# Block-sparse attention with a gated convolution FFN on one core: three stores change their queue, five are split, and the last 17 of 41 lines of a written-out order are replaced

## The chip, the core and the metric

One core of a Trainium2 chip. Its engines run instruction streams of their own and meet only at semaphores: TensorE (PE: matmuls; PEld its weight loads), VectorE (DVE), ScalarE (ACT), GpSimd (POOL) and SyncE (SP), which here only issues transfers and DMA transposes. The metric is the device time of one execution in microseconds (us), lower is better. Times of the trace count from the start of the profiled span.

## The reference

Four batches, eight heads, 768 tokens, head width 64. A query block of 32 tokens sees its neighbours, the first and last block and three drawn blocks; the softmax over those keys is followed by an FFN whose gate is a convolution over three tokens.

```python
scores = np.where(mask, scale * np.matmul(q, k.transpose(0, 1, 3, 2)), -1e9)
attn = np.exp(scores - np.max(scores, axis=-1, keepdims=True))
attn = attn / (np.sum(attn, axis=-1, keepdims=True) + 1e-09)
x = np.matmul(attn, v).transpose(0, 2, 1, 3).reshape(B, S, H * D)
h = np.maximum(x @ w_in, 0.0)
...
for k in range(K):
    conv_out += conv_w[k][None, None, :] * hp[:, k:k + S, :]
gate = 1.0 / (1.0 + np.exp(-conv_out))
out = h * gate @ w_out
```

## The kernel before

**Attention.** The heads are handled in 16 pairs (0 to 15, four to a batch). A unit is 1024 columns of scores, 144 units in all. PE writes a unit's scores into one of two PSUM buffers `st` in two halves of 512 columns (L773; the mask rides along as 24 more rows of the contraction), ScalarE takes their exponential into one of six buffers `pt` (L785), and PE multiplies that by the values in eight matmuls of 65 columns (L810). A unit's buffer `st` is free for the unit after next when its exponential is done. VectorE divides by the sums (`rcp` L719, `xtok` L721).

**FFN.** Tokens come in nine segments: 0 to 6 of 384 tokens (segment 4 is the first half of batch 2), then 7 (256 tokens) and 8 (128 tokens) for the second half of batch 3. For each, the attention's output is transposed (by DMA from SP, L730, for segments 2 to 6; by PE, L740, and a copy for 0, 1, 7 and 8), multiplied by `w_in` into one of two PSUM buffers `mix` (L910, called f1 here), and put through a relu on ScalarE (L930) or VectorE (L932). Segments 0 to 6 have eight groups g0 to g7 of one f1 and one relu each; 7 and 8 have four, g0 to g3. The gate takes four pairs p0 to p3 of feature chunks per segment: three multiplies (L968) and two adds (L976) on VectorE, a tanh on ScalarE (L1015), an add of one (g1, L1018) and a multiply (g2, L1023) on VectorE. In segment 8 the convolution runs on PE instead (L987, two steps per pair) with its tanh at L992.

**Output.** An output tile (b, t) is 128 tokens of batch b. It takes eight matmuls in four steps (L844, called f2 here; one step needs the g2 of one pair), is copied out of PSUM by ScalarE (L324) or VectorE (L328) into one of four buffers `o2s`, and stored (L854). Tiles (3,3), (3,4) and (3,5) are made in column pieces. A buffer of `o2s` is free again when its store has landed.

**The order.** No scheduler runs. The text `ORDER` (L20 to L61) lists all 1811 steps, two characters for the step, one for the engine where there is a choice, one for each buffer taken; `put_down` reads it and records the steps, so each engine's stream is exactly the list's order for that engine, and a step that waits holds up all behind it on its engine. A transfer's issue is a step of SP, ACT or POOL. `OUT_POOL` (L219) names three tiles whose store POOL issues; the others go to SP, and the third piece of a tile to ACT.

The loads of keys (`nat`), queries and values (`vn`) are issued by POOL (L239) in order; between them stand 1x1 copies (`pace`, L419) that wait for a given unit's exponential, so that loads start no sooner. Values go on by a copy to `vt` (L328) on VectorE.

Of the kernel before, what the change touches and what calls it, by code (L numbers as in the profile page):

```python
# [40 lines left out]
414213/24643lic41lplwlx3OVlqcj2lF1lz0cm0cnlGlAcu1cvcw1co4lBlHly3YV1lIlJV3cz1lClDV0cAcfcB3cE0lO1cFlPlL03ZVc540V1lQV  # L41
cG0lMlNAcgcJ1cKm70cO0cPckcllU1cpcqlVm8m9macr0cL5lR0lSmbcscQ2lWAlTAmf1mccx0cW1cycXcCc/0cDl+1l/d0cHcIcMcNcY4d41d5d13
d65mhmgmdmim0VcRcT2mjlX0lYcS1lZAcZd90c+m11dadh1d2dim40d3m2d7mkdb2dj3dm0dnm5d8dr1ds44454c4f4g04k4h4imemn2momlmqcUm3V
m6VmpkolKc61471lE4l048cVctdo1mJ1dcdw0dxdddk0dldt0dy4mv3mxmrmmmwde1mydfmzdB1dCdpmD0dqdJ0dKdumKdD5msdL3mA4t4u24d04y4j
mtdO1dvdPdzdAmEmudEdF1dT0dMdUdNmLmF49V2mBmCdQ1dV0dRdY1dSdZmMe40d+44bdge5e65dWmGmNV1mHV2dG2e91eadXd/eb3dH4eV2n21n3e0
e10e2ee0efeg1ej1m/0n0eke70e8n1A084aVn4V4mnn0nonq4nV3dI2e34z1mO4v4w4H4q4I34r1el0eo0ecepeq24M4x4E4F24J4K4Ledn50n6eh
n81n9ein7A9ew1exnb0nceB0ey5naVeCeD3emne1nfngAeG1eHeI14S4T0enereL0eMeN4nk1es1ezeAeEeFeJeKnleT1eUeOeP4oVndVanv1npnx
et1nD2nrnEeunwnseV0nmAeQ2eRnGnF4p4A4N0eSev4Onh0nieY0eZf11f2eW0njAbe+2nL3nynzmP1mQf35nAmRf60mV0f7f83eXmSe/fb1mWfcf0
f4f5mXfj0mYfk4sV34GV4nHnMntnI4BV4nOnNnPnu04CVfd4mTA3mZA0fl1nQfo1f9faoc1odo30feff1o4oeVnBnJo91fpfmfnft0oao5Afq0o60fu
o7fy1fzobAfg0nRnKfhnCnZ1fv2oz0oBnSo8Aor2oAosouotn+fG0oi0fHfA5fI3n/o0fL1fMo1A1fN4frfQ0fsof1fwfRfS1fxogfV1fWojohAfX0  # L50
ov4PV04QVoCfBfCfD2okVfJ0fKfOf+0f/ol1g61oo0g7opoH1oI4UV0g02owgb0gcfPfTfUfYfZfEoJoDoqVg85gd3oEg1g21omgg1g9ghnT0nUgl0
gagmnVoKonVoxoyo2mUfi04DfFgi4gn1g31oP3g4oFoLoGoRoQnWnXA1gt1gugegy0p11gfoX0gzgv0oYgjgkgogD1gEp2oMgA2gF5oSoToNoUgpgq0
oOgrgw0gxgBgCgM0gNgR1gSp3gGgHoZgT3gO4oVoWg5m+gsnYo+p4gW1gI2gJo/V3p0gP1gXpd0h30h4pep5V04Rp6mIgY1pfgK1h50gLA1pgphV1
h81h9pj1pkpm0pngQhd0ha2plA1cpoApH2hehm1gUhf5pIpKpJpLhnho4ps1gVpp0gZptpqg+hr0puAprAdg/1pP0pRpQhshw1py1hxh60h7pzhbpv0
pwpMht3h0pSpAApNpxAehF0hGp71pB0pChchgp8hhhp1p9pahqpTpX1pYpZhH1pDAfpUhy0p+hK0hLh10huhvpbA3h2AhzhApE1pO1hi0pVhjp/hk0
pFhT1hI0hM2hB2hChlVhD0pGApWhEVq0hJhUi00qq1hNqri1hV5q33q4q5q6q1q7qsAgi24q8hO1qw0i51qxhWi6ie0ifqH2hP1q2hXqb1qcq9qahY0
qIig3qyAhhZhQqX0qZqYqdqeqn0i31qoi4i70i8qfA0qpAiia2qKi90ihhR1iihSA2ibij1qz1qAqBikq+qt0ic1quidAqh1qvAjqih+0qjh/Vil0qk
imAru0rvqCqJqDqlA2rl1rmrwAqErnAq/qP3qRqLqFqGrr0rsrtAqMqQqNrx1ryro1rz1rAqOrBqSrprqArH0r30rIrC1rDr0rJ2rE1qmqgpcpirKqT
rFr1rGqUrLqVqWr4r91rarM0s70sd1rNses8sfs9rO1r5rPr2rQr6r7A3sarbrcsgrR0rSsbV2rdA0rTrUshVrVA1r8rescsirWrf1rgrhrirjArk
rX0rYrZr+s10s2s3s4s5Ar/Vs0s6  # L60
"""  # L61


# [19 lines left out]
class Graph:  # L83
# [29 lines left out]
def kernel(  # L113
# [32 lines left out]
    def many(n, shape, dt, tag):  # L146
        return [sb.tile(shape, dt, tag=f"{tag}{x}", name=f"{tag}{x}") for x in range(n)]
# [21 lines left out]
    o2s_t = many(NOS, [128, DM], FP32, "o2s")  # L169
# [18 lines left out]
    op = gr.op  # L188
# [23 lines left out]
    def T(u):  # L212
        return T0 + PACE0 * u if u < 18 else T0 + 18 * PACE0 + PACE1 * (u - 18)

    SW = 0.715
    NWARM, NFILL = 13, 29
    SPLIT = ()
    X_PE = (0, 1, 7, 8)
    OUT_POOL = ((2, 5), (3, 0), (3, 1))  # L219
    WOUT_U = (15, 19, 23, 27)  # L220


# [11 lines left out]
    def on(e):  # L234
        return {"SP": nc.sync, "ACT": nc.scalar, "POOL": nc.gpsimd}[e]
# [11 lines left out]
    def first_k(x, e, prio, after):  # L247
# [7 lines left out]
        out=sbi[64:MR], in_=sampled_blocks.bitcast(I32).rearrange("b r -> (b r)").unsqueeze(0).broadcast_to([NB, 6 * NB])),  # L255
# [8 lines left out]
        out=ident, in_=ident, compare_op=ALU.not_equal, fill=1.0, base=0,  # L264
# [10 lines left out]
    def a_edges(e):  # L275
# [8 lines left out]
        out=nblk.rearrange("j (b t) -> j b t", t=32),  # L284
        in_=ident[0:NB, 0:NB].unsqueeze(2).broadcast_to([NB, NB, 32])), -14, [o_ident])
# [36 lines left out]
    def dcopy(e, dst, src):  # L322
        if e == "ACT":
            nc.scalar.copy(out=dst, in_=src)  # L324
        elif e == "POOL":
            nc.gpsimd.tensor_copy(out=dst, in_=src)
        else:
            nc.vector.tensor_copy(out=dst, in_=src)  # L328
# [45 lines left out]
    for s in range(NHE):  # L374
# [372 lines left out]
    for u, (n, blocks) in enumerate(units):  # L747
# [3 lines left out]
        for part in range(2):  # L751
# [17 lines left out]
            def s_fn(e, stb=stb, pieces=pieces):  # L769
                st = st_t[stb.index]  # L770
                for (P, hh, kc, idx, x, n_) in pieces:
# [6 lines left out]
                        uses=[slot_b[P] for P in sorted({h[0] for h in heads})] + ([stb] if part else []))  # L778
# [49 lines left out]
    def out_block(b, t, due, deps, after, tail=False, last=False):  # L828
        gb, ob = gt_buf[b], Buf(P_os)
        halves = {3: ((0, 256), (256, 512)), 4: ((0, 256), (256, 384), (384, 512)),  # L830
                  5: ((0, 256), (256, 512))}.get(t if b == B - 1 else 0, ((0, 512),))
        outs = []
        for x, (c0, c1) in enumerate(halves):
            tl = last or x == 2
            mb = Buf(P_tail if tl else P_mix)

            def acc(mb=mb, c0=c0, c1=c1, tl=tl):
                t_ = st_t[mb.index] if tl else mix_t[mb.index]
                return t_[:, 0:c1 - c0]
            prev = None  # L840
            for a in range(4):
                def fn(e, a=a, acc=acc, c0=c0, c1=c1):
                    for ffc in (2 * a, 2 * a + 1):
                        nc.tensor.matmul(out=acc(), lhsT=gT_t[gb.index][:, ffc, 128 * t:128 * t + 128],  # L844
                                         rhs=woutb[:, ffc, c0:c1], start=(ffc == 0), stop=(ffc == NFFC - 1),
                                         skip_group_check=True)
                prev = op("f2", {"PE": 2 * t_mm(c1 - c0)}, fn, due + 0.4 * a + 0.1 * x,
                          [ld_wout[a]] + deps[a] + (last_exps if tl and a == 0 else []),
                          after=[prev] if a else after, alloc=[mb] if a == 0 else [], uses=[gb] + ([mb] if a else []))
            evo = op("ev", {"ACT": t_act(c1 - c0), "DVE": t_dps(c1 - c0) + 0.06},  # L850
                     lambda e, acc=acc, c0=c0, c1=c1: dcopy(e, o2s_t[ob.index][:, c0:c1], acc()),
                     due + 2.5, [prev], alloc=[ob] if x == 0 else [], uses=[mb] + ([ob] if x else []))
            by = "POOL" if (b, t) in OUT_POOL else "ACT" if x == 2 else "SP"
            outs.append(op("out", {by: {"POOL": SW, "ACT": 0.1, "SP": 0.5}[by]}, lambda e, c0=c0, c1=c1: on(e).dma_start(  # L854
                out=out[b, 128 * t:128 * t + 128, c0:c1], in_=o2s_t[ob.index][:, c0:c1]),
                due + 3, [evo], uses=[ob], dma=("sw" if by == "POOL" else "hw", 0.72 * (c1 - c0) / 512 + 0.05)))

    def whole_gate(n, heb, gtb, base, W):

# [30 lines left out]
    for n, (b, g, tok, C, _) in enumerate(SEGS):  # L890
# [8 lines left out]
        for fg in range(NFFC // FB):  # L899
            hb = Buf(P_mix)  # L900
            due = base + W * 0.6 * fg * FB / 8
# [33 lines left out]
            for f in range(FB * fg, FB * fg + FB):  # L935
                if f % 2 == 0 and tok + w1 < S:
# [4 lines left out]
                   uses=[hb] + ([] if new else [heb]) + (  # L941
                       [near[(n - 1, f // 2)] for f in range(FB * fg, FB * fg + FB) if f % 2 == 0] if g else []))
# [129 lines left out]
```

## Time and profile before

| | |
|---|---|
| median of 3 runs (lowest to highest) | 207.52 us (206.97 to 207.55) |
| the profiled execution's own time | 207.34 us |
| its span, first to last instruction | 205.5 us (so 1.84 us lie around it) |
| granted TensorE clock | 1.00 |
| transfers over the span | 25.45 MB, 124 GB/s |

Busy time on PE counts a matmul up to its modelled end, about 0.16 us past the point where the next one starts, so short waits of PE do not show as idle time. They show in the timeline, where rows of one kind follow each other: the distance of two starts against the columns that lie between them. In a row that merges several instructions the second number runs from the first start to the last end.

### The profile page before, as it was taken

Reading aid. Unit: us, or ns where it says so; the run is one execution under the profiler, and the core shown is the slowest. Engines: PE = TensorE matmul, PEld = TensorE weight load, DVE = VectorE, ACT = ScalarE, POOL = GpSimd, SP = SyncE. Lnnn points to the kernel's source line nnn. Section 1 sums busy time; section 2 is a strip of 40 time slices with the busy share of each in tenths; the row PEclk is TensorE's granted clock in tenths of the full one; section 3 lists DMA queues with packets and bytes.
Section 4 is the critical chain, followed back from the end, with each engine's and each line's share of the span. In section 5 each row is a group of like instructions: output and inputs, shape, how many; then the busy total and the mean of one; then the engine's idle time right before and its main releaser. Section 6 shows DMA issues by size and latency. Waiting matters only on the chain.

```text
span 205.5 us, 6316 instructions
## 1 busy us (share of the span) xinstructions
PE 199.5 (97%) x2442; PEld 144.4 (70%) x2442; DVE 186.5 (91%) x580; ACT 188.9 (92%) x249; POOL 62.7 (30%) x119
## 2 busy tenths in 40 slices
PE   6899999999999999999999999999999999999993
PEld 4688877877677766766477767756676757796773
DVE  6899999999999998999899979999999947999970
ACT  5999999999999999999799998999999979998751
POOL 6986735235241514114114554900000000000300
PEclk9999999999999999999999999999999999999999
DMA  6999999999959986999869496992041260010216
GB/s 146 186 195 198 195 197 130 145 114 139 159 79 111 147 122 84 244 121 168 199 97 176 60 134 94 211 169 58 2 132 21 75 218 10 3 53 3 102 59 200
DMA packets 50001, 25.45 MB, mean 124 GB/s; under 512 B 35508, under 2 KB 47380, under 8 KB 49972
## 3 DMA queue, kind: packets, MB, share of 16 engines
q0 software_dynamic: 20240, 12.03, 45.7%
q1 hardware_dynamic: 29300, 12.66, 31.4%
q8 instruction: 19, 0.31, 0.6%
q10 hardware_dynamic: 432, 0.36, 0.5%
q14 instruction: 10, 0.08, 0.2%
HBM read 23.09 MB, written 6.29 MB: 143 GB/s over the span
## 4 chain that ended last, share of the span: by engine, by line
PE 74%; ACT 13%; DVE 9%; issue 3%; ACTq 0%
PE st L773 26%; PE mix L910 16%; PE mix L844 14%; PE av L810 13%; ACT pt L785 8%; DVE m L968 3%; DVE t L328 2%; ACT m L1015 1%; PE st L844 1%; DVE m L976 1%; DVE xtok L721 1%; ACT hE L930 1%; PE mix L740 1%; ACT o2s L324 1%; PE av L987 1%
## 5 line engine op out<-in xcount | busy, mean ns | idle before, releaser
L785 ACT ACTIVATE pt<-st 128x1024 bf16<-128x1024 f32 x144 | 140.4, 1032 | 5.2 <-PE st L773 3.9
L773 PE MATMUL st<-t 88*128 88x256 bf16 (+2 forms) x600 | 92.9, 267 | 0.9 <-ACT pt L785 0.3
L810 PEld LDWEIGHTS <-pt 128*128 128x128 bf16 x1152 | 55.4, 97 | 13.7 <-ACT pt L785 0.5
L773 PEld LDWEIGHTS <-t 88*128 88x128 bf16 x600 | 48.7, 97 | 21.0 <-issue 1.6
L810 PE MATMUL av<-vt,pt 128*128 128x65 bf16 x1152 | 62.5, 193 | 0.1
L910 PE MATMUL mix<-xT,winb 128*128 128x384 bf16 (+2 forms) x288 | 55.4, 307 | 0.2
L968 DVE TENSOR_SCALAR m<-hE,cw 128x382 bf16<-128x382 bf16 (+2 forms) x192 | 50.3, 321 | 1.7 <-ACT hE L930 1.5
L844 PE MATMUL mix<-woutb,gT 128*128 128x512 bf16 (+2 forms) x200 | 49.0, 360 | 0.0
L976 DVE TENSOR_TENSOR m<-m 128x764 bf16<-128x764 bf16 (+2 forms) x64 | 33.7, 532 | 0.5
L910 PEld LDWEIGHTS <-winb 128*128 128x128 bf16 x288 | 23.6, 97 | 8.2 <-issue 0.9
L1015 ACT ACTIVATE m<-m 128x764 bf16<-128x764 bf16 (+2 forms) x32 | 26.2, 822 | 0.6 <-DVE m L976 0.5
L844 PEld LDWEIGHTS <-gT 128*128 128x128 bf16 x224 | 18.9, 97 | 9.5 <-DVE gT L1023 1.1
L419 POOL COPY pace<-pt 1x1 bf16<-1x1 bf16 x24 | 8.9, 370 | 49.8 <-ACT pt L785 49.6
L854 POOL DMA_DIRECT2D out_dram<-o2s x3 | 1.8, 590 | 59.0 <-ACT o2s L324 59.0
L930 ACT ACTIVATE hE<-mix 128x384 bf16<-128x384 f32 (+2 forms) x39 | 18.9, 501 | 0.2 <-PE mix L910 0.2
L1023 DVE TENSOR_TENSOR gT<-m,hE 128x764 bf16<-128x764 bf16 (+3 forms) x36 | 18.0, 510 | 0.7 <-ACT hE L930 0.4
L721 DVE TENSOR_TENSOR xtok<-av,rcp 128x384 bf16<-128x384 f32 (+2 forms) x36 | 18.2, 507 | 0.3
L239 POOL DMA_DIRECT2D nat<-in_q_dram x23 | 16.8, 730 | 1.7 <-issue 1.0
L328 DVE COPY t<-mix 64x384 bf16<-64x384 bf16 (+1 forms) x34 | 13.8, 411 | 0.6
L932 DVE TENSOR_SCALAR hE<-mix 128x384 bf16<-128x384 f32 x25 | 13.7, 550 | 0.6 <-PE mix L910 0.3
L328 DVE COPY o2s<-mix 128x512 f32<-128x512 f32 (+1 forms) x11 | 7.1, 654 | 6.3 <-PE mix L844 6.2
L1018 DVE TENSOR_SCALAR m<-m 128x764 bf16<-128x764 bf16 (+3 forms) x36 | 11.8, 334 | 0.6 <-ACT m L1015 0.5
(76 smaller groups left out, 132.3 us busy)
## 6 DMA issues: line engine op xcount, KB each, us to landing
out_dram<-o2s SPq DMA_DIRECT2D x18, 256.0 KB
vn<-in_v_dram POOLq DMA_DIRECT2D x16, 192.0 KB, 5.2
nat<-in_k_dram POOLq DMA_DIRECT2D x15, 192.0 KB, 4.5
nat<-in_q_dram POOLq DMA_DIRECT2D x6, 192.0 KB, 4.9
winb<-in_moe_w_in_dram POOLq DMA_DIRECT2D x2, 512.0 KB, 6.7
woutb<-in_moe_w_out_dram POOLq DMA_DIRECT2D x4, 256.0 KB, 6.0
nat<-in_q_dram POOLq DMA_DIRECT2D x9, 96.0 KB, 5.0
out_dram<-o2s POOLq DMA_DIRECT2D x3, 256.0 KB, 2.7
```

What stands on the lines that cost most here:

```text
L328: nc.vector.tensor_copy(out=dst, in_=src)
L721: nm = op("norm", {"DVE": t_dps(128 * C)}, lambda e: nc.vector.tensor_tensor(out=xtok_t[xk.index][:, 0:C].rearrange("p c h d -> p h c d"), ...
L773: nc.tensor.matmul(out=st[:, 128 * x:128 * (x + n_)], lhsT=t[0:88, 12 + 6 * hh + kc, :], rhs=t[0:88, idx:idx + (n_ - 1) * (2 if P < NPE el ...
L785: nc.scalar.activation(out=pt_t[ptb.index][:, c0:c1], in_=st_t[stb.index][:, c0:c1], func=AF.Exp, bias=0.0, scale=0.125)
L810: nc.tensor.matmul(out=o[:, off:off + 65], lhsT=pt_t[ptb.index][:, 128 * x:128 * x + 128], rhs=V_t[vslot_b[P].index][:, hh, kc, 0:65], sta ...
L844: nc.tensor.matmul(out=acc(), lhsT=gT_t[gb.index][:, ffc, 128 * t:128 * t + 128], rhs=woutb[:, ffc, c0:c1], start=(ffc == 0), stop=(ffc == ...
L910: nc.tensor.matmul(out=mix_t[hb.index][:, w1 * y:w1 * y + w1], lhsT=winb[:, fc, 128 * ffc:128 * ffc + 128], rhs=xT_t[xt_buf[n].index][:, f ...
L930: nc.scalar.activation(out=dst, in_=src, func=AF.Relu, bias=0.0, scale=0.5)
L968: nc.vector.tensor_scalar(out=m_t[cb.index][:, x, y, 0:w], in0=hE_t[heb.index][:, f0 + y, t0 + x:t0 + x + w], scalar1=cw[:, x, f0 + y:f0 + ...
L976: nc.vector.tensor_tensor(out=m[:, a_, :, 0:w], in0=m[:, a_, :, 0:w], in1=m[:, b_, :, 0:w], op=ALU.add)
L1015: th = [op("tanh", {"ACT": t_act(2 * w) + 0.04}, lambda e, cb=cb, w=w: nc.scalar.activation(out=m_t[cb.index][:, 0, :, 0:w], in_=m_t[cb.in ...
L1023: nc.vector.tensor_tensor(out=gT_t[gtb.index][:, f0:f0 + 2, t0:t1], in0=m_t[cb.index][:, 0, :, 0:w], in1=hE_t[heb.index][:, f0:f0 + 2, 1 + ...
```

## The change

The stores of tiles (2,5), (3,0) and (3,1) are issued by SP instead of POOL. The stores of (0,1), (0,2), (1,0), (1,1) and (1,2), 256 KB each, become two of 128 KB (columns 0 to 255 and 256 to 511), issued one behind the other by SP. The order is the same up to step 1100 of 1811 (about 118 us into the profiled span of before) and another one from there; the same 356 steps stand on PE behind that point.

```diff
-    OUT_POOL = ((2, 5), (3, 0), (3, 1))
+    OUT_TWO = ((0, 1), (0, 2), (1, 0), (1, 1), (1, 2))
...
-            by = "POOL" if (b, t) in OUT_POOL else "ACT" if x == 2 else "SP"
-            outs.append(op("out", {by: {"POOL": SW, "ACT": 0.1, "SP": 0.5}[by]}, lambda e, c0=c0, c1=c1: on(e).dma_start(
-                out=out[b, 128 * t:128 * t + 128, c0:c1], in_=o2s_t[ob.index][:, c0:c1]),
-                due + 3, [evo], uses=[ob], dma=("sw" if by == "POOL" else "hw", 0.72 * (c1 - c0) / 512 + 0.05)))
+            cuts = (c0, (c0 + c1) // 2, c1) if (b, t) in OUT_TWO else (c0, c1)
+
+            def store(e, cuts=cuts):
+                for y0, y1 in zip(cuts, cuts[1:]):
+                    on(e).dma_start(out=out[b, 128 * t:128 * t + 128, y0:y1], in_=o2s_t[ob.index][:, y0:y1])
+            by = "ACT" if x == 2 else "SP"
+            outs.append(op("out", {by: 0.1 if by == "ACT" else 0.5 * (len(cuts) - 1)}, store, due + 3, [evo], uses=[ob],
+                           dma=("hw", 0.72 * (c1 - c0) / 512 + 0.05)))
```

In `ORDER` 17 lines of text (L44 to L60) are replaced; read back, they differ in these places among others ("exp 108" is unit 108's exponential, "s4 p0" segment 4, pair 0):

| engine, place | before | after |
|---|---|---|
| ACT, units 106 to 113 | exp 106, exp 107, tanh s4 p0, exp 108, relu s4 g7, relu s4 g6, exp 109, exp 110, tanh s4 p1, exp 111, tanh s4 p2, exp 112, copy (1,4), copy (1,5), exp 113 | exp 106, exp 107, exp 108, relu s4 g6, tanh s4 p0, exp 109, relu s4 g7, exp 110, tanh s4 p1, exp 111, tanh s4 p2, exp 112, exp 113, copy (1,5) |
| DVE, same place | both adds of s4 p1 behind the last multiply of p2 and the first of p3 | both adds of s4 p1 ahead of them |
| DVE, first steps behind 118 us | value copy of pair 12 between two divisions; value copy of pair 13 28 steps later | value copy of pair 12, two key copies, relu s4 g0, value copy of pair 13, division of s5 |
| POOL, from 115 us | pace, keys 14, values 12, pace, three pieces of queries, two paces, keys 15, values 13 | values 12, pace, keys 14, a piece of queries, pace, pace, values 13, queries, pace, keys 15 |
| PE, f1 of s7 g0 | f1 first half, 4 matmuls of unit 141, f1 second half | f1 in one go, then unit 141 |
| ACT, last units | exp 140, relu s7 g1, exp 141, tanh s6 p3, ... | exp 140, exp 141, relu s7 g1, tanh s6 p3, ... |
| PE, s8 | f1 g3, g0, g2, conv p0 (both), f1 g1, conv p2, f2 (3,2), conv p2, ... | f1 g0, g2, conv p0, f1 g3, conv p0, f1 g1, conv p2 (both), f2 (3,2), ... |
| ACT, s8 | relu s7 g2, copy of xT (hp 3), copy (3,1), relu g3, tanh s7 p0, relu g0, relu g2, tanh s7 p1 | relu s7 g2, copy of xT (hp 1), tanh s7 p0, copy of xT (hp 3), copy (3,1), relu g0, relu g2, tanh s7 p1, relu g3 |
| SP, last stores | (3,2), (3,3), (3,5), (3,5), (3,4), (3,3), (3,4) from 199.5 us on | (3,0), (2,4), (2,5), (3,1) ahead of (3,3), (3,2), (3,4), (3,5), (3,5), (3,3), (3,4) |

Behind step 1100, five copies of output tiles move from VectorE to ScalarE (three of 512 columns, two of 256) and two of 512 columns the other way.

More of the change, by code (lines that the diff above doesn't have):

```diff
@@ L43 @@
 d65mhmgmdmim0VcRcT2mjlX0lYcS1lZAcZd90c+m11dadh1d2dim40d3m2d7mkdb2dj3dm0dnm5d8dr1ds44454c4f4g04k4h4imemn2momlmqcUm3V
[L44 to L57, printed above, removed]
@@ L58 @@
-imAru0rvqCqJqDqlA2rl1rmrwAqErnAq/qP3qRqLqFqGrr0rsrtAqMqQqNrx1ryro1rz1rAqOrBqSrprqArH0r30rIrC1rDr0rJ2rE1qmqgpcpirKqT
-rFr1rGqUrLqVqWr4r91rarM0s70sd1rNses8sfs9rO1r5rPr2rQr6r7A3sarbrcsgrR0rSsbV2rdA0rTrUshVrVA1r8rescsirWrf1rgrhrirjArk
-rX0rYrZr+s10s2s3s4s5Ar/Vs0s6
+m6VmpkolKc61471lE4l048cVctdo1mJ1dcdw0dxdddk0dldt0dy4mv3mxmrmmmwde1mydfmzdB1dCdpmD0dqdJ0dKdumKdD5msdL3mEdO1dvdzdAdE
+dF1dPmtmu4d04t4u2mAdT0dUdMmFdNmLdgdQ1dV0dRdY1mBmCmMdZmGe40dSe5mNV1dG2d+4dWdXm/1e91n04eV249V24aVn1V084j4y4q4r1e65
+mHA2eaee0d/e0eb2n50efn21n34mmO4sV3dHe10e24z1dI2eg3ej1ekn6e70eo0epn4Vnn0n7V9np4nV3no4oVel1eq04v4H4I34w4x4E4M4J4F24K
@@ new lines @@
+4Lne1e8ew1ecexn80n9ey5edeheieB0nfeCemenereG1eHnaAeD2ngAnb0es1ezeL0nceMeAnh1nv1nqet1eI34S4T0eN1eunrndVanwnD2nxnEny
+eT1eEeUnk0eFnieJeKeOePeY0nleV4eZnjAbnseQ2eRnGnz4pe3ev4AeS4N04Oe+0eW0f11nmAf2mP1eXmQe/mRf60f0f7mV0f35f4mSnAf82fb1mW
+nFnL3nMnHnBntnOnNmTV3nP4GV44BV4nu0nCnIfcfd1fj0mXfkf5mYfl4fo1f9oc1fpft0odmZA0nQfq0oeVnJo90fafufeoao31obAfg0nK4CVo4
+o5Afy1fzo60o7nZ1n+oz0nRfv3fA5o8AoAnSfhoBor1otosoC4PV0ouoDov4QVfG0fHff1n/o0fI2fL1fMoi0fmfnfQ0fRo1A1ojfrof1ogfsfN1fw
+fxfV1fWfS4okAohAoEoH2owfX0nT0ol1fBfCfJ0f+0f/g03fKomfOfPnUg61fTg7g85nVoIoxonVoJoyoFoKgb0gcoo1opfUfD1oLfYfZgg1ghg1nW
@@ new lines @@
+oqVfE4UV0gd2o2fi0m+4b4DfFmU4RoMgi1oP3oQg32oGoRoSg4oTgl0gmg21gn4p11g9gt1gugagep2gfgjgy0gkgzgogv0nXA1gA3oUgpgw0gxoX0
+gD1gEgM0gBoYgF5gq0groNoOoVoWgNgCp3oZgR1gSgO2gGgHgP1o+gT1o/A0p4gW0gXgY4h31h4gI1gJp5V3gK0pd1pepfpgh80gLV1gsg5nYh9gQ
+h50phA1p0mIp6ha3pj0pm1pkpnplA1cpoApH1pIpJpKhd1hehf5hm0pp0ps1pqptgUhnhr1gVprAdpuAgZpy0g+h60h7ho2pLpMpP0g/0pQpRpNpSh0
+hbhspv1hw0pzhcht1hxpwhghhpAApxAepThi2pX2pYhjp+pO1pZhy4hF1pB0pChGp71p8pDAfp9hK0h10pahp1hLhqhuhvhH0pUpVp/h2ApbA0hzhA
+hk0hB1hlVpE1pFhM3hChT1hD0hUi00hI0hJpGApWhEVq33q0q4q5q6q1qq1hNhP0hO1i1qw0qrhV5i22qsAgq7q8hWq2i51i6hXhY2ie0ifqH1q9qb1
@@ L61 @@
+qxqcqdqaig1qyAhhZqIqX0hQqKqYqeqn0qoi31i4i74i8qfA2qpAii90hR1ihiihSA2ia1ibqz2qAqBqCij0qDikqt0ic1quidAqh1qvAjqih+0qj
+h/Ail0qkqEimAqlA3rl0rmrnAqP3qQqFqJqGqLq+qSqRrr1rsrtAqMrx1ru0rvryro1rprH0rwArz2qNqTrAqOqZrBrIr30rqArC1rDr4r91raqgpc
+piqmqUrE1rJ2q/qVr0rFqWrGr1rKrM1sd0s71rNrbr5s8serO3r2rLrPrcrQrdA2s9r6r7V0rR1rSsfrTrUsasgrf0rgrVA1sbA3shArer8rWscsirh
+rirjArkrX1rYrZr+s11r/Vs0s2s3s4s5As6
 """
```

## The prediction

> **What bounds the kernel now.** I read the page first, then the busy time by stage behind the point from which the two orders differ, then PE's timeline there.
>
> ```profile
> span 205.5 us, 6316 instructions
> PE 199.5 (97%) x2442; PEld 144.4 (70%) x2442; DVE 186.5 (91%) x580; ACT 188.9 (92%) x249; POOL 62.7 (30%) x119
> ...
> out_dram<-o2s POOLq DMA_DIRECT2D x3, 256.0 KB, 2.7
> ```
>
> ```profile
> 118.00:130.00 12.00, 12.00 (x147) 8.32 (x144) 10.52 (x26) 11.03 (x14) 6.50 (x12) 1.00 1.00 124
> ...
> 150.00:170.00 20.00, 20.00 (x228) 13.56 (x225) 16.35 (x44) 18.61 (x24) 0.00 (x0) 1.00 0.37 117
> ...
> 186.00:202.40 16.40, 16.04 (x176) 12.29 (x174) 13.16 (x56) 10.78 (x26) 1.75 (x3) 1.00 0.26 91
> 202.40:205.50 3.10, 0.00 (x0) 0.00 (x0) 0.00 (x0) 0.23 (x1) 0.00 (x0) 0.98 0.39 117
> ```
>
> The columns are PE, PEld, DVE, ACT and POOL busy, the clock, the transfers' share and GB/s. Of the stages shown PE has a hole in the last two alone, 0.36 us up to 202.4 and then 3.1 us in which the last store lands. The change takes no matmul away, so it can win only what PE loses between matmuls, which the busy time hides. PE's timeline shows it, in six places:
>
> ```profile
> 134.28 1.22 PE L773 MATMUL st<-t 88*128 88x128 bf16 x8
> 135.34 0.28 PE L810 MATMUL av<-vt,pt 128*128 128x65 bf16 x4
> ...
> 140.63 0.83 PE L773 MATMUL st<-t 88*128 88x128 bf16 x4
> 141.30 0.40 PE L810 MATMUL av<-vt,pt 128*128 128x65 bf16 x8
> ```
>
> ```profile
> 185.64 1.03 PE L844 MATMUL mix<-woutb,gT 128*128 128x512 bf16 x4
> 186.63 0.60 PE L910 MATMUL mix<-xT,winb 128*128 128x256 bf16 x4
> ...
> 188.16 0.28 PE L810 MATMUL av<-vt,pt 128*128 128x65 bf16 x4
> 188.52 0.60 PE L910 MATMUL mix<-xT,winb 128*128 128x256 bf16 x4
> ...
> 190.44 0.59 PE L844 MATMUL mix<-woutb,gT 128*128 128x512 bf16 x2
> ...
> 190.98 0.59 PE L844 MATMUL mix<-woutb,gT 128*128 128x512 bf16 x2
> 191.49 1.80 PE L910 MATMUL mix<-xT,winb 128*128 128x128 bf16 x24
> 193.37 0.50 PE L987 MATMUL av<-hE,diag 128*128 128x130 bf16 x6
> ```
>
> Four matmuls of 512 columns take 1.03 us and two 0.59, so a matmul costs (1.03 - 0.59) / 2 = 0.22 us for 512 columns, 0.42 ns a column, once its tail is left out. Against that price: the eight scores from 134.28 are four halves of a unit, 2048 columns or 0.86 us, and the next row starts after 1.06: **0.20 lost**. The four from 140.63 are 1024 columns, 0.43 of 0.67: **0.24**. The four f2 from 185.64 need 0.87 of 0.99: **0.12**. Four matmuls of 65 columns (0.03 each) from 188.16 need 0.12 of 0.36: **0.24**. Two f2 from 190.98 need 0.43 of 0.51: **0.08**. The 24 f1 of 128 columns need 1.29 of 1.88: **0.59**. Together 1.47 us, the ceiling of what a new order can win.
>
> **The change part by part.**
>
> *Stores to SP.* Three issues leave POOL, which does nothing from 150 to 170 us and only them behind 186 (1.75), and come to SP.
>
> ```profile
> L854 SPq DMA_DIRECT2D out_dram<-o2s x24: 332/412/575, 81.2 to 202.4; - x24
> ```
>
> ```profile
> 199.47 3.29 SPq L854 DMA_DIRECT2D out_dram<-o2s  x7
> ```
>
> At 0.41 us each that is 1.2 us of SP. SP's new stream has them ahead of the last seven, behind the copy of (3,0). That copy is done at 187.96 (its row, from 187.37, follows below) and SP's last seven begin at 199.47: cost nothing. Without that idle SP they would delay the last stores by 1.2 us at most. The buffers: (2,5) has its store now when (3,0) has been copied, about 188.5, and lands by 191.2 with the 2.7 of the page; the next user of a buffer comes at 198.5.
>
> POOL's issues could also have slowed VectorE beside them.
>
> ```profile
> 188.75 1.25 DVE L968 TENSOR_SCALAR m<-hE,cw 128x256 bf16<-128x256 bf16 x6
> ...
> 192.18 0.92 DVE L968 TENSOR_SCALAR m<-hE,cw 128x256 bf16<-128x256 bf16 x4
> ```
>
> ```profile
> 192.49 1.75 POOL L854 DMA_DIRECT2D out_dram<-o2s  x3 [59.00 <-ACT o2s L324]
> ```
>
> The multiplies under POOL's stores (from 192.49) take 0.23 each, those before them 0.21 (0.92 / 4 against 1.25 / 6): at most 0.08 us in four. I put it at zero. [...]
>
> *Split stores.* Five more issues at 0.41 us are 2.1 us of SP.
>
> ```profile
> 95.98 5.89 SPq L854 DMA_DIRECT2D out_dram<-o2s  x4
> 103.42 1.19 SPq L730 DMA_TRANSPOSE xT<-xtok  x1
> ```
>
> Four of the five lie here or just behind; after the row of four SP is free from 101.87 to 103.42, so three halves' 1.2 us just fit, and no transpose starts later. The bytes are the same. Cost between 0 and, if the gap did not hold, 0.4 for the transpose at 103.42; zero taken.
>
> *The order, first place (131 to 142 us).* Both losses there are scores that wait for an exponential.
>
> ```profile
> 131.10 1.95 ACT L785 ACTIVATE pt<-st 128x1024 bf16<-128x1024 f32 x2
> 133.10 0.84 ACT L1015 ACTIVATE m<-m 128x764 bf16<-128x764 bf16 x1
> 133.85 1.01 ACT L785 ACTIVATE pt<-st 128x1024 bf16<-128x1024 f32 x1
> 134.75 0.87 ACT L930 ACTIVATE hE<-mix 128x384 bf16<-128x384 f32 x2
> ...
> 137.63 0.84 ACT L1015 ACTIVATE m<-m 128x764 bf16<-128x764 bf16 x1 [0.19 <-DVE m L976]
> ...
> 140.01 1.02 ACT L785 ACTIVATE pt<-st 128x1024 bf16<-128x1024 f32 x1
> ```
>
> Exp 108 (133.85) stands behind a tanh, exp 112 (140.01) behind all of these and a wait for VectorE's add. In the new order exp 108 follows exp 107 at once. Start to start an exp takes 1.95 - 1.02 = 0.93, a tanh 133.85 - 133.10 = 0.75, a relu 0.37 (two in 0.87 with a tail of 0.50). From exp 107 (131.10 + 0.93 = 132.03): exp 108 starts at 132.96 and ends at 133.97, against 134.85 now, so unit 110's scores do not wait: 0.20 won. Up to exp 112 the new list has five exp, three tanh, two relu: 132.03 + 4.65 + 2.25 + 0.74 = 139.67, end 140.69, provided that the adds, which the new VectorE stream has two multiplies earlier, are there. PE wants it 0.24 + 0.20 earlier than the present end of 141.03, at 140.59, so up to 0.10 of the 0.24 may stay: 0.14 to 0.24 won. Sum **-0.4**; if the lead is lost again, 0.
>
> *Second place (182 to 188.5 us).* Exp 141 now goes ahead of a relu, so unit 143's scores, the relu of s7 g3 and f1 of s7 g0 and g2 come sooner. The losses of 0.12 and 0.24 hang on these relus:
>
> ```profile
> 187.37 0.59 ACT L324 COPY o2s<-mix 128x512 f32<-128x512 f32 x1
> 187.84 0.63 ACT L930 ACTIVATE hE<-mix 128x512 bf16<-128x512 f32 x1
> ```
>
> ACT's work between is unchanged, so of the second I take half: **-0.2**, bounds 0 and -0.36.
>
> *Third place, s8.*
>
> ```profile
> 191.17 0.27 ACT L324 COPY xT<-mix 128x128 bf16<-128x128 bf16 x1 [0.93 <-PE mix L740]
> 191.61 0.59 ACT L324 COPY o2s<-mix 128x512 f32<-128x512 f32 x1 [0.17 <-PE mix L844]
> 192.13 0.39 ACT L930 ACTIVATE hE<-mix 128x256 bf16<-128x256 f32 x1
> ```
>
> The first conv needs the relu of g0. Before, relu g3 (192.13) and a tanh go first, and conv starts at 193.37 behind three f1. In the new order g0's relu is the one at 192.13, done at 192.52. A tanh now stands ahead of the copy at 191.17, up to 0.5 us on f1 g0; but g2's bank is freed by the copy of (3,1), 192.20, in either order, so 0.2 of that is hidden and f1 g2 runs from 192.24 to 192.67. Conv starts there without a wait, f1 g3 follows, and at 193.10 the same work is done as before at 193.37: **-0.27**; bounds +0.1 (all of the tanh shows) and -0.59.
>
> *Copies that change engine.* ScalarE gets one 512-column copy more and two of 256, VectorE has these less: about 0.47 + 2 x 0.28 = 1.0 us by the distance of starts, 187.37 to 187.84 for the first and by columns for the others. They fall where ACT has room, 1.0 of 12, 1.4 of 20 and 5.6 of 16.4 us: nothing.
>
> The sum is -0.4 - 0.2 - 0.27 = -0.87. Some twenty other steps of PE have leads of 0.05 to 0.2 us in the new list by the same counting, so I give 0.17 back: **-0.7**. The profiled execution took 207.34 (205.5 and 1.84 around it), 0.18 under the median: 206.6 on its own scale, **206.8** against 207.52.
>
> **The rivals.**
>
> *Values come late (slower).* VectorE's stream now has the value copy of pair 13 in front of two divisions and the relu of s4 g1, not behind all these. By the count of PE's columns PE wants that relu's bank at 126.7.
>
> ```profile
> 124.07 0.35 DVE L328 COPY vt<-vn 128x768 bf16<-128x768 bf16 x1
> ```
>
> ```profile
> 118.88 0.61 POOL L419 COPY pace<-pt 1x1 bf16<-1x1 bf16 x1 [0.89 <-ACT pt L785]
> ...
> DMA to landing us min/median/max: 3.4/5.2/10.1
> ```
>
> That load is issued behind two paces, about 119.9. Copy, two divisions, a reciprocal and the relu take about 1.9, so it must land by 124.8: 4.9 us. At 3.4 nothing happens, at 5.2 PE loses 0.3, at 7 it loses 2.1 and the time is 208.9; slower than before from 5.6 on. For it: the median. Against it: no other load of that size is issued in the three us ahead, so I expect 4.2.
>
> *The leads do not hold:* waits come back elsewhere, above all behind the copies of (2,2) and (2,5) on ScalarE, 0.47 each: 207.1 to 207.7.
>
> *All six losses go:* -1.3: 206.2.
>
> *SP is late:* halves and stores push transposes back by 0.4 to 1.2: 207.3 to 208.2.
>
> **How the numbers follow.** Forecast 0.48, leads lost 0.20, values late 0.16, SP 0.08, all six 0.08. A difference of 0.3% (0.62 us) is what a measurement here can tell from none, so 206.9 is the edge: of the forecast 0.38 lie below it. Faster 0.46, same 0.33 (0.10 of the forecast, all of the lost leads, 0.03 of the late values), slower 0.21. The forecast's own range is 206.4 to 207.3; eight in ten need 206.1 (ceiling of 1.47) to 208.3 (part of the late values).
>
> **What would show it.** Right: scores of units 110 and 114 follow their predecessors without the 0.20 and 0.24; first conv of s8 directly behind f1 g2; last PE row ends near 201.6; SP has room before its last seven. Wrong: PE losing time at 126 to 128 with VectorE idle before a value copy; transposes at 103 us later than now; new losses between 142 and 182, where before has none.

## The result, and the profile after

| | median us | executions | ratio to before, 95% interval |
|---|---|---|---|
| before | 207.59 | 22 | |
| after | 206.95 | 22 | 0.9966 [0.9952, 0.9979] |
| after, measured once more (below: e6_again) | 207.04, before beside it 207.39 | 12 and 35 | 0.9991 [0.9974, 1.0008] |

By the medians the change wins 0.64 us in the first comparison and 0.35 in the second, whose interval does not rule out that nothing was won; 206.8 was forecast. The profiled execution of after took 207.02.

The page of after, first lines, and the busy time by stage (the columns as in the prediction):

```profile
span 205.2 us, 6315 instructions
PE 200.1 (98%) x2442; PEld 145.2 (71%) x2442; DVE 184.7 (90%) x577; ACT 189.4 (92%) x252; POOL 60.0 (29%) x116
```

```profile
186.00:202.40 16.40, 16.08 (x176) 12.35 (x174) 12.89 (x54) 11.20 (x28) 0.00 (x0) 1.00 0.30 108
202.40:205.20 2.80, 0.00 (x0) 0.00 (x0) 0.00 (x0) 0.09 (x1) 0.00 (x0) 0.83 0.42 126
```

POOL's 1.75 us of stores are gone from the last stages, and from 202.4 to the end it is 2.8 us, not 3.1. PE is as full as before; what changed is again between matmuls. PE's timeline of after at the two places of the first part, and ScalarE's:

```profile
135.28 0.60 PE L773 MATMUL st<-t 88*128 88x256 bf16 x4
135.72 0.60 PE L844 MATMUL mix<-woutb,gT 128*128 128x512 bf16 x2
...
141.11 0.38 PE L773 MATMUL st<-t 88*128 88x384 bf16 x2
141.33 0.28 PE L810 MATMUL av<-vt,pt 128*128 128x65 bf16 x4
```

```profile
131.49 2.92 ACT L785 ACTIVATE pt<-st 128x1024 bf16<-128x1024 f32 x3
...
139.97 1.96 ACT L785 ACTIVATE pt<-st 128x1024 bf16<-128x1024 f32 x2
```

Unit 110's scores (135.28) take 0.44 to the next row, the price of 1024 columns; the first half of unit 114's (141.11) takes 0.22 for 512. The 0.20 and 0.24 are gone: exp 106, 107 and 108 run in a row of three. The last stage:

```profile
185.30 1.46 PE L844 MATMUL mix<-woutb,gT 128*128 128x512 bf16 x6
186.67 1.03 PE L914 MATMUL mix<-xT,winb 128*128 128x256 bf16 x8
...
188.11 0.40 PE L810 MATMUL av<-vt,pt 128*128 128x65 bf16 x8
188.56 0.60 PE L914 MATMUL mix<-xT,winb 128*128 128x256 bf16 x4
...
191.06 0.59 PE L844 MATMUL mix<-woutb,gT 128*128 128x512 bf16 x2
191.68 1.25 PE L914 MATMUL mix<-xT,winb 128*128 128x128 bf16 x16
192.77 0.33 PE L991 MATMUL av<-hE,diag 128*128 128x130 bf16 x3
```

The first convolution (192.77) follows its f1 at once. Six f2 take 1.37 where 1.29 are needed (0.08 lost, 0.12 before), the eight from 188.11 0.45 for 0.24 (0.21, was 0.24), two f2 0.62 for 0.43 (0.19, was 0.08), 16 f1 1.09 for 0.86 (0.23; 24 lost 0.59 before). And two losses above 0.1 us are new:

```profile
119.54 0.29 PE L810 MATMUL av<-vt,pt 128*128 128x65 bf16 x4
119.83 0.60 PE L844 MATMUL mix<-woutb,gT 128*128 128x512 bf16 x2
...
158.15 0.29 PE L810 MATMUL av<-vt,pt 128*128 128x65 bf16 x4
158.45 0.60 PE L773 MATMUL st<-t 88*128 88x256 bf16 x4
```

Four matmuls of 65 columns cost 0.12; here 0.29 and 0.30 pass, so 0.16 and 0.18 are lost. The f2 at 119.83 waits for VectorE's gate product, the scores at 158.45 for an exponential.

**A stretch without chance.** Single times spread over more than the effect, and the trace shows where from. The exponential of unit 79, in before, in after, and in the last experiment:

```profile
97.31 1.03 ACT L785 ACTIVATE pt<-st 128x1024 bf16<-128x1024 f32 x1
```

```profile
97.52 1.03 ACT L785 ACTIVATE pt<-st 128x1024 bf16<-128x1024 f32 x1
```

```profile
97.16 1.03 ACT L784 ACTIVATE pt<-st 128x1024 bf16<-128x1024 f32 x1
```

In the 14 profiles it starts between 97.03 and 99.23 us, though little ahead of it differs but the form of some stores. In the second look at after, whose profiled execution took 207.86, PE waits there for keys and queries (1.04 us, ended by VectorE's copy):

```profile
57.67 0.41 PE L809 MATMUL av<-vt,pt 128*128 128x65 bf16 x8
59.12 0.38 PE L772 MATMUL st<-t 88*128 88x384 bf16 x2 [1.04 <-DVE t L327]
```

At this place PE loses 1.7 us in e4_tail's profile, 1.2 here, 0.6 in e12_fixold's and under 0.25 in the others. So I compare the stretch from exp 79 to the end, worked out from the starts and ends in the one trace that each kernel left: 108.21 us before, 107.64 after and 107.66 in its second look. That is -0.56, of which -0.34 lie between exp 79 and the last matmul's start (104.80 to 104.46) and -0.22 behind it (3.40 to 3.18), in what is called the close here. All runs in that measure, us:

| run | ratio, 95% interval | exp 79 to last matmul | last matmul to end | sum |
|---|---|---|---|---|
| before | | 104.80 | 3.40 | 108.21 |
| after | 0.9966 [0.9952, 0.9979] | 104.46 | 3.18 | 107.64 |
| e1_stores | 0.9992 [0.9971, 1.0014] | 104.78 | 3.10 | 107.88 |
| e2_order | 0.9957 [0.9938, 0.9977] | 104.28 | 3.44 | 107.72 |
| e3_first | 0.9972 [0.9956, 0.9988] | 104.60 | 3.10 | 107.70 |
| e4_tail | 0.9978 [0.9961, 0.9995] | 104.63 | 3.18 | 107.81 |
| e5_exp108 | 1.0007 [0.9988, 1.0025] | 105.06 | 3.10 | 108.16 |
| e6_again | 0.9991 [0.9974, 1.0008] | 104.48 | 3.18 | 107.66 |
| e7_copy | 0.9980 [0.9967, 0.9992] | 104.41 | 3.17 | 107.58 |
| e8_all | 0.9972 [0.9949, 0.9996] | 104.21 | 3.16 | 107.38 |
| e9_whole | 0.9979 [0.9964, 0.9994] | 104.29 | 3.46 | 107.75 |
| e10_shift | 0.9966 [0.9946, 0.9986] | 104.38 | 3.18 | 107.55 |
| e12_fixold | 0.9944 [0.9924, 0.9964] | 104.00 | 3.48 | 107.48 |
| e13_late | 0.9943 [0.9924, 0.9961] | 103.76 | 3.18 | 106.94 |

Where an expectation says what PE loses behind 118 us, it is the sum over all matmuls there of the time from start to start beyond the cheapest of their shape: 3.18 before, 2.83 after. Its level hangs on the price taken as the cheapest (1 ns on each of about 1000 matmuls is 1 us), the difference of 0.35 does not.

### The profile page after: what moved, and what is told of

It is laid out like the page before. It is cut to its first block, busy times and chain, and to the rows that moved or that the text cites. A ratio compares the mean times of both kernels' runs of the same rounds, so it can differ in the third digit from the quotient of the medians.

```text
span 205.2 us, 6315 instructions
## 1 busy us (share of the span) xinstructions
PE 200.1 (98%) x2442; PEld 145.2 (71%) x2442; DVE 184.7 (90%) x577; ACT 189.4 (92%) x252; POOL 60.0 (29%) x116
## 4 chain that ended last, share of the span: by engine, by line
PE 78%; ACT 14%; DVE 4%; issue 3%; ACTq 0%
PE st L773 25%; PE mix L914 18%; PE mix L844 15%; PE av L810 13%; ACT pt L785 10%; PE av L230 2%; DVE t L328 2%; ACT hE L934 2%; ACT m L1019 1%; PE st L844 1%; PE mix L740 1%; PE av L991 1%; ACT o2s L324 1%; DVE diag L391 1%; PE mix L536 1%
## 5 line engine op out<-in xcount | busy, mean ns | idle before, releaser
L844 PE MATMUL mix<-woutb,gT 128*128 128x512 bf16 (+2 forms) x200 | 49.6, 360 | 0.0
L914 PEld LDWEIGHTS <-winb 128*128 128x128 bf16 x288 | 24.1, 97 | 8.6 <-issue 0.7
L419 POOL COPY pace<-pt 1x1 bf16<-1x1 bf16 x24 | 7.6, 317 | 50.3 <-ACT pt L785 50.1
L239 POOL DMA_DIRECT2D vn<-in_v_dram x16 | 11.5, 720 | 1.3 <-issue 0.6
L328 DVE COPY t<-stg 64x1536 bf16<-64x1536 bf16 x20 | 11.6, 586 | 0.3
```

What stands on the lines that cost most here:

```text
L239: return op(name, {eng: occ}, lambda e: on(e).dma_start(out=dst(), in_=src), prio, deps, dma=(kind, service), **kw)
L914: nc.tensor.matmul(out=mix_t[hb.index][:, w1 * y:w1 * y + w1], lhsT=winb[:, fc, 128 * ffc:128 * ffc + 128], rhs=xT_t[xt_buf[n].index][:, f ...
```

## The experiments

Each is one kernel with its own profile. "The new store code" is that of the diff, "the old" that of before. Steps in `ORDER` are moved by hand; the buffers stay as they are. The blocks below name the steps instead of printing `ORDER`'s letters.

**e1_stores, e2_order: the stores alone, the order alone.**

```diff
 after, with
-ORDER = after's
+ORDER = before's          (e1_stores)

 before, with
-ORDER = before's
+ORDER = after's           (e2_order)
```

> Before's order with the new store code: all whole stores on SyncE, five of them in halves, no other step moved. Theory order (the gain lies in the order of the last 85 us alone): same as before, ratio 0.999 to 1.001, PE loses 0.19 at 134.7, 0.23 at 140.7 and 0.24 before the first convolution as before. Rival stores (POOL's issues slowed VectorE in the last stage, or the halves drain earlier): 0.3 us or more is won here, ratio 0.9985 or lower, and the multiplies at 192 us get shorter than 0.23 us each.

> After's order with the old store code: three stores on GpSimd, none in halves. Theory order: the whole gain, 0.6 to 0.7 us, ratio 0.9965 with its interval. Rival stores: less than 0.35 us, ratio above 0.9983.

Order alone: ratio 0.9957, -0.52 up to the last matmul, and the loss of 0.18 at 158 is not there; PE loses 2.64. The stores alone change nothing between matmuls (104.78 against 104.80, PE loses 3.16), so the whole gain on PE is the order's. Four multiplies at 192 us take 0.88 us without POOL's stores beside them, 0.92 with them, which PE does not feel. But the end comes 0.30 us sooner behind the last matmul. The rival of the stores had named 0.3 us, from a faster VectorE or from halves that land earlier; the gain is neither of these (why, below at e9_whole). In the times e1_stores cannot be told from before. Last store and header line in e2_order, then in after:

```profile
core 0 of [0], span 204.9 us
...
202.02 0.35 ACTq L853 DMA_DIRECT2D out_dram<-o2s  x1
```

```profile
core 0 of [0], span 205.2 us
...
202.52 0.36 ACTq L857 DMA_DIRECT2D out_dram<-o2s  x1
```

From the end of that issue it is 204.9 - 202.37 = 2.5 us with the old stores and 205.2 - 202.88 = 2.3 with the new.

**e3_first, e4_tail: one stretch of the new order.** The first 1310 steps of before's list in after's order and then before's; the first 1683 of after's list in before's order and then after's. Both have the new store code, so e1_stores is what they compare with.

```diff
-ORDER = after's, whole
+ORDER = after's up to 141 us, before's behind it      (e3_first)
+ORDER = before's up to 188.5 us, after's behind it    (e4_tail)
```

> New store code; the steps up to 141 us in after's order, the rest in before's. Theory order: PE's waits of 0.19 for exp 108 and 0.23 for exp 112 go, the new one of 0.16 at 119.6 comes, the six places behind 186 us lose what they lose in before: 0.25 to 0.3 us won, ratio 0.9987. Rival give-back (a lead of PE is spent on the next wait, since ScalarE and VectorE are nearly full): PE is back at before's time by 165 us, ratio 0.9995 to 1.000.

> New store code; before's order up to 188.5 us, after's behind it. Theory order: PE loses 0.6 us between 188.5 and 194 where before loses 0.8, no wait before the first convolution, 0.2 us won, ratio 0.999. Rival (the new tail needs the earlier relus of the middle stretch): nothing won, ratio 1.000, and the first convolution waits for relu g0 as before.

e3_first gains 0.18, less than the 0.25 to 0.3 expected, all on PE: the two waits go, the 0.16 at 119.6 and one of 0.05 at 132.5 come, and behind 142 us PE loses what it lost before, to 0.01 us at each place. The lead is not given back. e4_tail gains 0.15 up to the last matmul, the first convolution does not wait, but its close is 0.08 longer (3.18 against 3.10), which all kernels with after's tail and the new stores show: there SyncE issues its last store 0.36 us behind the last matmul's start, not 0.25. Both intervals are too wide to see this in the times.

**e5_exp108: the first swap alone.** The store code is the new one, so this too compares with e1_stores.

```diff
-... exp 107, tanh s4 p0, exp 108, relu s4 g7 ...
+... exp 107, exp 108, tanh s4 p0, relu s4 g7 ...
```

> Before's order with one step moved, exp 108 ahead of the tanh that stood in front of it, and the new store code. Theory one swap wins the first wait: PE's 0.19 at 134.7 goes, the 0.23 for exp 112 stays as it is, PE loses 0.19 less in all. Rival ScalarE sets the end (up to exp 112 it has the same work as before, so PE only comes earlier to the second wait): the 0.19 goes, the wait for exp 112 grows from 0.23 to about 0.42, PE loses as much as before in all.

Neither theory holds: 0.28 us are lost against e1_stores.

```profile
135.10 0.28 PE L809 MATMUL av<-vt,pt 128*128 128x65 bf16 x4
135.78 1.46 PE L843 MATMUL mix<-woutb,gT 128*128 128x512 bf16 x5 [0.39 <-ACT hE L933]
```

```profile
134.51 0.83 ACT L1018 ACTIVATE m<-m 128x764 bf16<-128x764 bf16 x1
135.24 0.87 ACT L933 ACTIVATE hE<-mix 128x384 bf16<-128x384 f32 x2
```

The scores no longer wait at 134.5, but the relus now stand behind exp 108 and the tanh (135.24), and the f2 that takes their bank waits for them; exp 112's wait shrinks only from 0.23 to 0.10. The new order moves more than this: one relu stands ahead of the tanh, and the copy of (1,4) behind unit 112 is gone from ScalarE.

**e6_again, e9_whole, e10_shift: the new wait at 158.** ScalarE in after:

```profile
152.52 1.98 ACT L785 ACTIVATE pt<-st 128x1024 bf16<-128x1024 f32 x2
154.81 1.94 ACT L785 ACTIVATE pt<-st 128x1024 bf16<-128x1024 f32 x2 [0.31 <-ACT pt L785]
```

Exp 122 (154.81) starts 0.31 us after exp 121 ended, in a stretch where ScalarE has no other hole. Is it chance, or what stands ahead of it?

```diff
 after, unchanged                                              (e6_again)

-    OUT_TWO = ((0, 1), (0, 2), (1, 0), (1, 1), (1, 2))
+    OUT_TWO = ()                                              (e9_whole)

+                if u == 79:
+                    nc.scalar.activation(out=pt_t[ptb.index][:, 0:1], in_=st_t[stb.index][:, 0:1], func=AF.Exp, bias=0.0,
+                                         scale=0.125)          (e10_shift)
```

> The changed kernel once more, as a second look. Theory chance: the 0.185 at 158.2, which the order with the old stores did not show, is not there, the other waits behind 118 us come back within 0.02 us each, and what PE loses behind 118 us is 2.64 as with the old stores, not 2.83. Rival stores: the 0.185 is there again and belongs to the new store code.

> After with no store in halves; the three stores stay on SyncE. Place in ScalarE's stream: in after, its record 319 (the 128th behind record 191) is exp 122, which starts 0.32 us after the semaphore instruction ahead of it, where 0.045 is usual, and PE then waits 0.19 at 158.2; with the old stores exp 122 is record 318 and on time. Theory place by the halves: the halves add a semaphore instruction to ScalarE, so without them exp 122 is record 318, on time, and the 0.19 goes. Rival queue: the move of the three stores to SyncE brings it, and exp 122 stays record 319 and late. In time 0.2 us at most, ratio 0.9955 to 0.9966.

> After with one exponential of one column more on ScalarE (unit 79's first column computed again, same result) in its idle 1.1 us at 98.5: every later record of ScalarE moves back by one. Theory place: exp 122 becomes record 320 and starts within 0.06 us of its semaphore instruction, PE's wait of 0.19 at 158.2 goes although ScalarE has more to do, PE loses 2.64 behind 118 us. Rival wait (exp 122 is late for its scores or a buffer): exp 122 starts 0.3 late as before and the 0.19 stays.

Not chance: in e6_again the hole (0.30) and PE's 0.19 are back, and so they are with the copy moved (e7_copy: 0.32 and 0.20). In e9_whole both are gone:

```profile
152.04 3.96 ACT L785 ACTIVATE pt<-st 128x1024 bf16<-128x1024 f32 x4
```

Four exponentials without a hole, and 104.29 to the last matmul, as with the old stores (104.28). So the halves cost 0.18 us on ScalarE and PE, not the queue. The ratio missed what was expected (0.9979, not 0.9955 to 0.9966): too small a difference for the times, and e9_whole loses 0.28 behind the last matmul, of which more below. How the halves do it: the records of an engine in the trace, counted from 0, include its semaphore instructions, which wait for another engine or a transfer. For three records of ScalarE, the time since the semaphore instruction ahead of them ended:

```
                 record 63   record 191   record 319, what it is, time since
after             0.36 us      0.32 us    exp 122     0.32 us   (PE +0.18)
e6_again          0.37         0.32       exp 122     0.32      (PE +0.19)
e2_order          0.36         0.32       semaphore instruction
e9_whole          0.37         0.32       semaphore instruction
e10_shift         0.36         0.32       exp 123     0.34      (PE +0.16)
e13_late          0.36         0.32       semaphore instruction
other exponentials that had only such an instruction to wait for: 0.045
```

The records 63, 191 and 319 stand 128 apart in every run. At 63, at 191 and in e10_shift the exponential ahead was still running as well; from start to start two exponentials take 0.93 us, and by that count these three began 0.23 to 0.25 us late, exp 122 in after 0.28. Before has exp 122 at 319 as well, but ScalarE was still busy with a tanh, which hid it. e10_shift missed its number: with the added exponential ScalarE's stream has fewer semaphore instructions, and exp 122 became record 317, not 320. It started on time (0.045), exp 123 fell on 319 and was late, and PE's wait stayed. That speaks for the place and not for exp 122. That the halves bring the extra instruction follows from e9_whole; in before's order, too, exp 122 is record 319 without them and 320 with them (e1_stores). Which of the five does it wasn't tried.

e9_whole also has the long close, 3.46, with all stores on SyncE. All ten profiles with the stores on SyncE and five of them in halves have 3.10 to 3.18, the four others 3.40 to 3.48. The semaphore records behind the last matmul show two different reasons. First SyncE waits for all transfers, in nine steps in a fixed order of semaphores; then POOL closes the program with seven short records. In us from the last matmul's start:

```
               last store seen   SyncE's waits    POOL's record 196, time since     end
               landed by SyncE   all done         the record ahead of it
before              2.20             2.24              0.38                        3.40
e2_order            2.27             2.31              0.33                        3.44
e12_fixold          2.28             2.32              0.35                        3.48
e9_whole            2.29             2.63              (POOL ends at 192)          3.46
after               2.31             2.34              (POOL ends at 192)          3.18
e1_stores           2.23             2.27              (POOL ends at 191)          3.10
```

With the three stores on POOL its stream is longer and its last records reach number 196, which starts 0.33 to 0.38 us behind the one ahead, where the other closing records take 0.03 to 0.07. In before it is another instruction than in the other two, and nothing is left to wait for. Without these stores POOL's stream ends before it. Record 68, 128 earlier, is late in all 14 profiles: 0.42 to 0.44 us after its semaphore instruction, the other `pace` copies that only waited so at most 0.09. That is ScalarE's pattern on a second engine.

In e9_whole SyncE is late instead. The issues of SyncE and ScalarE take eight landing semaphores in turn, by the semaphore number that each record names (before and after). Before has 88 such issues and after 96, so the last store has the same semaphore in both, and SyncE's last wait is for it. e9_whole has 91: its last store has the semaphore of the fourth wait, and five more waits of 0.06 us each follow. So in these runs the short close (3.10 to 3.18) took both: no stores on POOL, and a number of issues that left the last store's semaphore at the end of SyncE's nine waits. Another number of halves wasn't tried.

**e7_copy, e8_all, e12_fixold, e13_late: can it be beaten?** Ahead of the changed lines, in before and after alike, PE waits 0.32 for VectorE's copy at 98 and 0.14 for the gate behind it. The gate's pairs are counted through here: pairs 9, 10 and 11 are p1, p2 and p3 of segment 2.

```diff
 VectorE at 96.7 us
-... g2 pair 9, reciprocal, +1 of pair 10, +1 of pair 11, copy t, g2 pair 10 ...
+... g2 pair 9, copy t, reciprocal, +1 of pair 10, +1 of pair 11, g2 pair 10 ...   (e7_copy, e8_all)
+... g2 pair 9, copy t, reciprocal, +1 of pair 10, g2 pair 10, +1 of pair 11 ...   (e12_fixold)
+... g2 pair 9, reciprocal, +1 of pair 10, copy t, g2 pair 10, +1 of pair 11 ...   (e13_late)
 PE at 119.5 us, in the last three
-... f2 of (1,2), second half of unit 95's values ...
+... second half of unit 95's values, f2 of (1,2) ...
 PE at 153.7 us, in e8_all
+... second half of unit 122's scores ahead of the first of unit 119's values ...
 stores
 old code                                                                          (e12_fixold)
+    OUT_TWO = ((2, 3), (2, 4), (2, 5), (3, 0), (3, 1))                            (e13_late)
```

> After with one step moved that stands before the changed lines: VectorE's copy of transposed queries and keys at 98.1 us goes ahead of a reciprocal and two additions for the gate, for which ScalarE's tanh is late. Theory order: PE's waits of 0.32 and 0.14 at 98.4 and 99.3 go, 0.45 us won on after, ratio to before 0.9945 to 0.995. Rival give-back: the gate's multiply comes later and f2 waits 0.3 to 0.5 instead, same as after, 0.9966.

> As the run with the copy moved, and f2 at 119.8 goes behind one half of attention times values, which is ready, and the second half of scores 122 ahead of one. Theory order: 0.13 of the 0.16 at 119.6 goes as well, nothing else moves, ratio to before 0.994. Rival give-back: as the run with the copy alone.

> After's order with the old store code, VectorE's copy at 98.1 ahead of the reciprocal and both additions, the gate's multiply (g2 of pair 10) ahead of the second addition, and f2 at 119.8 behind the ready half of attention times values. Theory: against the order with old stores the waits of 0.32 and 0.14 at 98 shrink to under 0.1 together (with the copy moved alone 0.40 came back at f2, whose multiply stood behind two additions) and 0.11 of the 0.16 at 119.6 goes: 0.45 us less, ratio to before 0.9935 to 0.9945. Rival give-back: the second f2 group waits for its later multiply by the same amount, ratio 0.996.

> After's order with VectorE's copy at 98.1 us behind the first addition for the gate and ahead of its multiply (g2 of pair 10), f2 at 119.8 behind the ready half of attention times values, and the five halves moved to stores behind 185 us: (2,3), (2,4), (2,5), (3,0), (3,1). Theory: the halves' semaphore instruction stands behind exp 122 in ScalarE's stream, so exp 122 is record 318 and on time and the 0.19 at 158.2 is gone; the waits at 98 fall from 0.46 to 0.1, at 119.6 from 0.16 to 0.05; from the last store's issue to the end it takes 2.2 to 2.3 us as with the halves before, not 2.5. Ratio to before 0.9925 to 0.9940. Rival close (the short close belongs to halves of the early stores): 2.5 to the end, 0.25 us of it lost again. Rival queue: five more issues on SyncE push the last stores back, 0.4 us or more lost at the end.

e7_copy wins 0.06 on after: the scores no longer wait, but f2 behind them waits 0.40 for g2 of pair 10, which the move had put behind copy and both additions. That rival was right in kind, the ratio is above both numbers. e8_all wins 0.26 on after, ratio 0.9972 and not the 0.994 expected: 0.11 at 119.6, of which 0.05 come back one step later, and 0.13 at 158 (exp 122 is still record 319, but its scores come earlier). e12_fixold still waits 0.27 at that f2: its ratio is the one expected, but up to the last matmul it wins 0.28 on e2_order where 0.45 was expected. In e13_late PE runs through; first after, then e13_late:

```profile
97.75 1.03 PE L844 MATMUL mix<-woutb,gT 128*128 128x512 bf16 x4
98.94 0.61 PE L773 MATMUL st<-t 88*128 88x384 bf16 x4 [0.16 <-DVE t L328]
99.52 1.25 PE L844 MATMUL mix<-woutb,gT 128*128 128x512 bf16 x5
```

```profile
97.39 1.03 PE L843 MATMUL mix<-woutb,gT 128*128 128x512 bf16 x4
98.25 0.60 PE L772 MATMUL st<-t 88*128 88x384 bf16 x4
98.69 1.46 PE L843 MATMUL mix<-woutb,gT 128*128 128x512 bf16 x6
```

The scores take 0.58 there and 0.44 here, with 0.86 for the four f2 ahead of them, not 1.19. Five other halves keep the short close (96 issues again) and put no extra semaphore instruction ahead of exp 122. e13_late has the lowest median of all, 206.03 against 207.47 for before beside it, ratio 0.9943 [0.9924, 0.9961], a shade over the 0.9940 expected, and 106.94 on the stretch: 0.70 less than after, 1.27 less than before. SyncE has the room:

```profile
186.99 14.70 SPq L856 DMA_DIRECT2D out_dram<-o2s  x15
```

The row ends at 201.69, after's (below) at 202.73, both 0.76 us behind the last matmul's start: the rival of a crowded SyncE is refuted.

## Why the prediction was right, and where not

**Forecast and sum.** -0.7 was forecast; the two medians give -0.64 and -0.35, the stretch -0.56. The mechanism, PE's waits between matmuls, is shown by e1_stores and e2_order: all that PE wins, it wins by the order. The forecast was to come from PE alone, though, and PE won 0.34, half of it; the other 0.22 came behind the last matmul, where the sum has no term. That the total lies near 0.7 is in part luck. One sign fell short with it: PE's last row ends at 202.19, 0.14 sooner than before, or 0.35 when the 0.21 that this execution lies later is taken off, and not near 201.6. The other signs came: the two waits gone, the first convolution behind its f1, and SyncE idle from 192.7 to 198.7 ahead of its last seven stores.

**Stores to SP, split stores: "cost nothing", "zero taken".** Right for SyncE, wrong in the parts of the sum. SyncE in after:

```profile
96.19 6.36 SPq L857 DMA_DIRECT2D out_dram<-o2s  x7
103.64 1.19 SPq L730 DMA_TRANSPOSE xT<-xtok  x1
...
188.03 14.70 SPq L857 DMA_DIRECT2D out_dram<-o2s  x11
```

The three halves fit as counted, and the transpose at 103.64 is no later than 103.42 was, for all of this execution lies 0.21 later. But this step looked only at the issuing queues and at VectorE. The stores' form reached two other places: -0.22 in the close and +0.18 at exp 122. Their sum is near the zero taken, by luck. Without POOL's 1.75 us VectorE's four multiplies took 0.04 less and PE won 0.02 (e1_stores): POOL's issues beside VectorE had next to no price here.

**First place, -0.4.** Right at the place: 0.42 less at the two scores; with the new losses ahead of them e3_first nets 0.18. But the text put the first 0.20 down to exp 108's place alone, and e5_exp108 shows that this place alone loses 0.28.

**Second place, -0.2.** The size holds by luck, the place does not. The waits named lost 0.05 and 0.02 less. What is left of the order's 0.52 without e3_first's 0.18 and e4_tail's 0.15 is 0.19; three waits of 0.04 to 0.05 at 149, 152 and 164 that the prediction did not list went, and 0.07 came at 180.7. The f1 at 188.56 still waits for a relu that follows exp 142 and the copy of (3,0) on ScalarE, as before: that exp 141 goes first moved nothing there.

**Third place, -0.27, bounds +0.1 and -0.59.** -0.20 between 188.5 and 194: the convolution's 0.24 went, of g2's wait 0.31 became 0.20, and the tanh showed 0.11 at f1 g0, as the text had feared in part.

**The 0.17 given back** for short leads stands for one wait in the main: 0.16 at 119.6. The new order asks for VectorE's product before it is there (e8_all shows that the order of PE's steps alone gets 0.11 of it back, of which 0.05 are lost again a step later).

**Values late.** The load landed 4.1 us after its issue (4.2 expected), and the copy came behind the relu without a wait:

```profile
vn<-in_v_dram POOLq DMA_DIRECT2D x1, 192.0 KB, 4.1
```

```profile
124.13 0.56 DVE L936 TENSOR_SCALAR hE<-mix 128x384 bf16<-128x384 f32 x1 [0.28 <-PE mix L914]
124.72 0.36 DVE L328 COPY vt<-vn 128x768 bf16<-128x768 bf16 x1
```

What a later landing would cost wasn't tried.

**Leads lost.** New losses between 142 and 182 us were named as a sign of it, and one came, at 158. But it was not a lead spent elsewhere, nor the copies on ScalarE: it came with the store code.

## What to carry to other kernels

When an engine is 97% busy, compare start to start with the cheapest of each shape: waits that the busy time hid made all that PE gained here, and from exp 79 to the last matmul they repeated to 0.02 us (104.46 in after, 104.48 in e6_again) while the time itself spread by 0.5 and more. Measure from an instruction behind the chance (here PE's wait at 58 us, under 0.25 to 1.7) to the end. And cost an edit on every engine whose stream it touches: splitting five transfers here added a semaphore instruction to ScalarE, which issues none of the five, and shifted everything behind it; and three stores taken off POOL shortened the end of POOL's stream by 0.3 us.

## What was not expected of the hardware

On two engines records that stand 128 apart start late. On ScalarE records 63 and 191 began 0.32 to 0.37 us after the semaphore instruction ahead of them in all 14 profiles, and so did 319 in the five where it was an exponential that could have begun before; other exponentials that waited for such an instruction alone took 0.045. On POOL it is record 68 (0.42 to 0.44 in all 14 profiles, like copies up to 0.09) and record 196 in the three whose stream is long enough. It cost 0.18 us at exp 122 and about 0.3 in the close, and one instruction more or less ahead decided what stood at the place (in before's order exp 122 is record 319, with the halves 320). The step of 128 records and the price are these traces'; what makes the starts late is not shown, nor that an execution without the profiler has them.

From the last matmul's start to the end it took 3.10 to 3.18 us or 3.40 to 3.48, by which queue issued the stores and how many issues there were in all.
